# Casting loads behind the selector and masks: a new instruction order at the head of a windowed-attention and MLP kernel

## The chip, the cores and the metric

The kernel runs on one core of one Trainium2 chip. A core has a matrix engine (TensorE, PE in the profile), a vector engine (VectorE, DVE), an activation engine (ScalarE, ACT), GpSimd (POOL) and SyncE (SP), which only starts transfers. ScalarE and GpSimd can start transfers too. The metric is the device time of one execution in microseconds; lower is better.

## The reference

Four batches, 8 heads, 768 positions, head size 64. Attention with a window of 128 and 4 sink positions comes first, then a residual MLP over the rows of 512 values:

```python
scores = scale * np.matmul(q, k.transpose(0, 1, 3, 2))
keep = is_sink | in_window            # in_window: 0 <= row - column < 128
a = softmax(np.where(keep, scores, -1e9)); x = np.matmul(a, v)   # heads side by side: 768 x 512

tok = np.einsum('ts,bsd->btd', w_tok, alpha1 * x + beta1)
u = x + lam * tok
ch = np.maximum((alpha2 * u + beta2) @ w_ch1, 0.0) @ w_ch2       # 512 -> 2048 -> 512
return u + lam * ch
```

Inputs and output are float32; the kernel multiplies in float16.

## The kernel before

The work is cut into some 1,140 tasks, numbered in the order in which the function's body adds them. Three written tables say how they are emitted. `ORDER` lists the task numbers; each engine runs its own share of the list strictly in that order. `ENGINES` has one digit per task for the engine that runs it (0 ACT, 1 DVE, 2 PE, 3 POOL, 4 SP). `HOMES` has one digit per buffer and says in which of the fixed places of its kind it lies: two buffers with one home wait for each other. `IDLES` puts multiplications of a zero tile (`warm`, L148) ahead of some tasks, so that TensorE does not stand idle. Nothing is decided at run time: an instruction waits for its data or its buffer, and all that is queued behind it on its engine waits too.

In batch 0 the order around the change is this, with the names that the profile shows:

- **Loads of q and k.** `load_qk` loads a block of one of q (t = 0) and k (t = 1) for a pair of heads hp (393 KB in float32). Blocks of pair 0 are float32 loads of SyncE (L402, tile `nat`) and are cast by VectorE (`n`, L157). The six blocks of pairs 1 to 3 are in the set `CASTING`: GpSimd starts loads that turn them into float16 on the way (L395). Below, k11 is the k block of pair 1, q10 the q block of pair 1, and so on.
- **Transposes.** `trans` turns a block with TensorE (tile `tp`; L512 for pair 0, L509 for the others; both need the identity `iden`, which GpSimd makes at L330 and L331), and VectorE or ScalarE copies the result into `qkT`.
- **Small constants of GpSimd.** The block masks `mask0` and `maskn` (five selects, L338 to L346), the selector `sel` with the small identity `iden8` (L370, L374), the sink mask `bm` (L359, L363) and `iden`.
- **Scores, sinks and values.** S (L617, L622, L683, L686), the exponential E on ScalarE (L644, L691), sinks `sk` (L554), the products `pv` with v (L716, L723), their division `x` on VectorE (L748, L749), then `xh`, x times `la_b`, on GpSimd (L758).
- **w_tok.** Six loads of SyncE (L440, `wtn`), cast to `wt` on ScalarE or VectorE (L819, L821), transposed (L814, `wT`), used by the token product `tok` (L854). wt_0 is the first of them.
- **w_ch1.** GpSimd loads it in four casting quarters (L453, `w1f`). The hidden layer `h` (L934) multiplies with it: tiles 4 to 7 need the second quarter, 8 to 11 the third, 12 to 15 the fourth. A tiny load, `gates` (L460), makes SyncE wait for a quarter, so that w_ch2 (L449) and the q, k and v of batch 1 come after it.

Later batches repeat attention and MLP, the attention of one batch between the multiplications of the MLP before it.

The functions that start the moved loads are these; the tables themselves are shown with the change.

Of the kernel before, what the change touches and what calls it, by code (L numbers as in the profile page):

```python
# [77 lines left out]
def kernel(  # L78
# [119 lines left out]
    for r in range(NR):  # L198
# [18 lines left out]
        26, 6, 9, 7, 10, 5, 11, 8, 18, 15, 72, 19, 1, 12, 3, 0, 4, 2, 22, 14, 73, 74, 45,  # L217
        48, 46, 17, 39, 49, 47, 53, 13, 40, 50, 41, 90, 95, 43, 91, 51, 54, 103, 52, 16, 44,
        61, 104, 42, 96, 109, 100, 62, 107, 110, 63, 55, 28, 108, 92, 56, 101, 21, 68, 65,
        59, 93, 20, 69, 97, 102, 111, 94, 24, 98, 57, 60, 30, 112, 105, 23, 58, 99, 113,  # L220
        128, 106, 114, 116, 25, 131, 135, 78, 115, 64, 27, 138, 31, 32, 117, 132, 29, 129,
        136, 33, 122, 66, 125, 34, 123, 137, 119, 139, 126, 35, 79, 70, 120, 140, 124, 84,
        71, 80, 133, 130, 141, 67, 146, 85, 134, 121, 147, 144, 75, 118, 158, 86, 154, 148,
        159, 145, 142, 87, 149, 150, 155, 160, 143, 76, 88, 151, 156, 81, 77, 166, 152, 162,
        167, 89, 127, 82, 163, 213, 83, 168, 209, 164, 165, 214, 210, 153, 217, 179, 211,
        178, 157, 197, 229, 36, 212, 215, 218, 185, 216, 226, 230, 219, 176, 161, 177, 220,
        169, 223, 222, 232, 225, 224, 221, 227, 237, 233, 279, 238, 234, 228, 273, 280, 182,
        171, 204, 257, 274, 175, 277, 258, 200, 231, 259, 278, 246, 260, 295, 199, 384, 241,
        248, 188, 186, 291, 296, 247, 172, 243, 289, 174, 181, 242, 293, 292, 187, 170, 290,
        267, 37, 294, 271, 358, 268, 198, 285, 349, 272, 381, 301, 286, 366, 351, 303, 302,  # L230
        189, 297, 378, 173, 304, 281, 180, 352, 203, 249, 190, 282, 298, 379, 250, 287, 380,
        192, 353, 385, 288, 206, 283, 386, 369, 375, 367, 265, 284, 368, 202, 370, 266, 363,
        376, 371, 253, 377, 201, 299, 254, 372, 364, 183, 382, 191, 300, 373, 615, 365, 275,
        374, 383, 357, 261, 276, 408, 262, 387, 263, 184, 409, 205, 195, 239, 411, 264, 410,
        395, 269, 396, 240, 397, 270, 196, 388, 614, 621, 235, 412, 400, 194, 244, 398, 236,
        401, 255, 617, 251, 245, 256, 389, 390, 399, 252, 311, 359, 207, 193, 391, 424, 616,
        335, 425, 393, 341, 426, 392, 336, 648, 427, 634, 413, 394, 312, 636, 414, 428, 419,
        404, 420, 415, 360, 405, 313, 429, 208, 422, 337, 416, 361, 441, 421, 622, 402, 314,
        423, 442, 626, 403, 305, 638, 315, 406, 430, 640, 316, 435, 431, 306, 641, 355, 436,
        443, 619, 437, 338, 649, 618, 438, 362, 317, 432, 637, 407, 307, 433, 345, 444, 339,  # L240
        439, 635, 318, 445, 450, 434, 639, 644, 319, 451, 628, 452, 620, 440, 308, 645, 340,
        453, 417, 446, 323, 447, 418, 320, 309, 448, 324, 321, 658, 322, 329, 449, 642, 659,
        454, 325, 625, 643, 330, 646, 347, 455, 326, 623, 343, 647, 464, 344, 456, 465, 348,
        466, 460, 457, 467, 650, 327, 458, 331, 461, 629, 459, 472, 462, 632, 463, 653, 356,
        651, 656, 627, 332, 38, 654, 480, 333, 342, 624, 652, 473, 310, 476, 468, 471, 470,
        469, 481, 474, 488, 885, 477, 475, 482, 492, 655, 490, 493, 350, 483, 478, 514, 491,
        516, 489, 657, 479, 515, 660, 517, 630, 882, 665, 518, 663, 354, 328, 666, 502, 880,
        661, 664, 498, 879, 519, 508, 499, 346, 503, 678, 662, 512, 509, 679, 504, 513, 487,
        484, 671, 485, 676, 486, 506, 677, 877, 548, 505, 672, 680, 507, 526, 549, 546, 527,
        631, 334, 522, 674, 681, 528, 547, 907, 523, 534, 903, 529, 633, 682, 675, 878, 542,  # L250
        683, 535, 890, 689, 543, 550, 685, 684, 690, 510, 551, 494, 511, 673, 667, 544, 495,
        668, 891, 496, 686, 545, 901, 687, 669, 497, 693, 888, 688, 883, 530, 694, 670, 700,
        531, 524, 897, 701, 698, 500, 691, 525, 696, 699, 552, 501, 697, 704, 553, 558, 695,
        705, 904, 692, 562, 559, 706, 909, 887, 707, 563, 564, 898, 708, 702, 566, 565, 910,
        715, 703, 567, 532, 716, 889, 713, 533, 709, 714, 896, 520, 710, 556, 717, 521, 538,
        557, 537, 540, 539, 536, 560, 541, 899, 718, 921, 572, 922, 881, 711, 574, 884, 573,
        576, 712, 561, 719, 902, 577, 575, 555, 727, 720, 569, 908, 721, 580, 728, 578, 722,
        581, 729, 554, 723, 905, 730, 568, 739, 724, 579, 725, 592, 570, 911, 726, 582, 740,
        593, 588, 912, 583, 595, 584, 571, 906, 743, 589, 731, 585, 900, 590, 732, 605, 744,
        587, 733, 596, 606, 734, 607, 611, 594, 597, 602, 745, 612, 586, 613, 599, 895, 603,  # L260
        591, 757, 765, 600, 758, 601, 759, 766, 741, 771, 760, 742, 916, 772, 751, 917, 746,
        773, 752, 913, 761, 919, 774, 886, 767, 918, 604, 762, 763, 598, 768, 777, 764, 779,
        920, 923, 780, 914, 755, 915, 778, 608, 756, 926, 930, 735, 609, 931, 924, 927, 781,
        736, 925, 775, 782, 737, 928, 753, 929, 893, 738, 934, 754, 892, 769, 935, 932, 610,
        941, 770, 819, 776, 942, 894, 939, 820, 821, 940, 937, 936, 823, 749, 822, 945, 748,
        824, 938, 747, 827, 933, 948, 950, 750, 952, 943, 951, 825, 953, 787, 828, 944, 807,
        788, 797, 826, 808, 949, 946, 829, 798, 801, 954, 830, 791, 802, 956, 947, 792, 783,
        955, 957, 963, 961, 784, 789, 958, 962, 811, 790, 964, 959, 785, 812, 965, 805, 786,
        795, 806, 960, 967, 796, 799, 793, 968, 966, 970, 972, 794, 813, 971, 969, 815, 973,
        814, 809, 800, 816, 803, 810, 974, 978, 804, 976, 979, 837, 975, 977, 835, 838, 980,  # L270
        841, 836, 839, 842, 818, 843, 840, 845, 981, 832, 982, 846, 817, 986, 844, 831, 990,
        987, 983, 988, 847, 991, 984, 851, 833, 992, 1002, 993, 834, 848, 855, 852, 985,
        849, 1003, 859, 856, 1004, 989, 1006, 850, 860, 1005, 853, 998, 1007, 1008, 868,
        999, 857, 1009, 997, 865, 995, 858, 862, 996, 869, 866, 1000, 874, 994, 854, 1001,
        1016, 863, 875, 1040, 1017, 1038, 1041, 1032, 1039, 871, 1020, 872, 1028, 1021,
        1011, 1024, 1029, 1013, 1018, 1033, 1012, 1025, 1034, 1019, 1036, 1010, 1035, 1042,
        1037, 1076, 1043, 1070, 1077, 870, 1074, 1071, 1054, 1075, 1022, 1055, 1060, 1023,
        1048, 1061, 1058, 1049, 1066, 1059, 1014, 1044, 1015, 1067, 1072, 1045, 1056, 1073,
        1026, 1057, 1078, 1068, 1079, 1064, 1069, 1046, 1027, 1050, 1063, 1047, 1052, 1082,
        1053, 1051, 1084, 1083, 1062, 1065, 1030, 1085, 1080, 1101, 1031, 1081, 1091, 1102,  # L280
        1107, 1092, 1097, 1093, 1103, 864, 1108, 1105, 867, 1098, 1111, 1106, 1104, 1113,
        1112, 1089, 1114, 1115, 1086, 1116, 1090, 861, 1094, 1087, 1117, 1099, 1109, 1100,
        1121, 1095, 1110, 1125, 1118, 1122, 1124, 1134, 1126, 1123, 1128, 1135, 1127, 1119,
        1136, 1088, 1140, 1120, 873, 876, 1131, 1129, 1141, 1096, 1137, 1142, 1132, 1130,
        1133, 1138, 1139,
    )
    ENGINES = (
        "3313134433443333444444444444444433334441111201201202120212021213030121211201211210200200"
        "2020201202011202020202020213213213213213213202002020202020213121312131213121312131404444"
        "4044413314433334411114413334444042213221321021020121021021321202020020211212021212020212"  # L290
        "1212020202120212120212020202120202020212122221022221422221022221422221022221013111111131"
        "1311333333302002002102132002132002102020101212010321213120301212131201012121312010121213"
# [17 lines left out]
        "1202002102135312330203"  # L310
    )
    IDLES = (
        (73, 0, 65), (46, 0, 12), (49, 1, 1), (90, 3, 10), (61, 3, 2), (109, 3, 3), (92, 3,
        1), (166, 1, 4), (162, 0, 1),
    )
    W1_SINCE = 20000.0
# [1011 lines left out]
```

## Time and profile before

| what | value |
|---|---|
| time, median of 3 runs | 255.22 us (254.76 to 255.94) |
| the profiled execution's own time | 255.43 us |
| its span, first to last instruction | 253.2 us |
| TensorE busy | 245.4 us, 97% of the span |
| VectorE, ScalarE, GpSimd busy | 190.7, 133.3 and 102.2 us |
| granted TensorE clock | full (1.000) |
| read from memory, written to it | 29.91 MB, 6.29 MB |

The page gives busy time for each engine over the whole span; one line cuts the span in 40 slices and gives each engine's busy share in tenths. The chain of work that ended last follows, from the last instruction back, what released each step. The timeline lists an engine's instructions in order of time: start, length, engine, line, operation, and in brackets how long the engine had been idle and what ended that. "Landing" of a transfer is when its semaphore says that all of it is there.

### The profile page before, as it was taken

The page shows a single profiled execution, that of the slowest core. Times are in us where ns is not written, and L with a number is a line of the kernel's source. Part 1 is how long each engine was busy: PE and PEld are TensorE (multiplying, and loading weights), DVE is VectorE, ACT ScalarE, POOL GpSimd, SP SyncE. Part 2 cuts the span into 40 slices and gives each one's busy share as a digit, 9 for nine tenths or more (in the row PEclk, how much of TensorE's full clock was granted, in tenths as well). Part 3 has the DMA queues.
Part 4 walks back from the last instruction along what each step waited for, and adds up shares of the span by engine and source line. Part 5 has one row for each costly group of instructions (what it writes and reads, how often), then busy time and mean ns, then how long its engine had stood idle before and what let it go on. Part 6 is the DMA issues. An engine that isn't in the chain of part 4 may idle for free.

```text
span 253.2 us, 5499 instructions
## 1 busy us (share of the span) xinstructions
PE 245.4 (97%) x2167; PEld 159.8 (63%) x2167; DVE 190.7 (75%) x402; ACT 133.3 (53%) x219; POOL 102.2 (40%) x124
## 2 busy tenths in 40 slices
PE   8699999999999999999999999999999999999993
PEld 7555646676545544566687686567677676667882
DVE  5588987877788874978879986577778983228892
ACT  2499925879976034787932535566660235543000
POOL 8317854895247417525682040065562220000010
PEclk9999999999999999999999999999999999999999
DMA  6999999999979998997485674420000140100317
GB/s 170 207 240 292 229 276 311 330 362 285 221 130 250 247 194 158 192 244 168 107 176 117 114 151 124 132 66 0 3 0 3 38 83 7 41 0 3 122 70 268
DMA packets 86129, 38.79 MB, mean 153 GB/s; under 512 B 73540, under 2 KB 80460, under 8 KB 86104
## 3 DMA queue, kind: packets, MB, share of 16 engines
q1 hardware_dynamic: 66576, 28.06, 46.9%
q10 hardware_dynamic: 15784, 7.11, 11.9%
q0 software_dynamic: 3744, 3.28, 8.3%
q8 instruction: 17, 0.28, 0.5%
q14 instruction: 8, 0.07, 0.1%
HBM read 29.91 MB, written 6.29 MB: 143 GB/s over the span
## 4 chain that ended last, share of the span: by engine, by line
PE 94%; DMA 3%; DVE 0%; SPq 0%; issue 0%
PE h L934 33%; PE P L1051 22%; PE tok L854 12%; PE ch L1119 8%; PE pv L723 5%; PE S L622 4%; DMA nat<-in_k_dram 3%; PE S L617 2%; PE tp L512 1%; PE pv L716 1%; PE tp L509 1%; PE wT L814 1%; PE sk L554 1%; PE idle L148 1%; PE uTp L895 1%; PE pv L609 1%
## 5 line engine op out<-in xcount | busy, mean ns | idle before, releaser
L934 PE MATMUL h<-uT,w1f 128*128 128x384 f16 x512 | 89.6, 327 | 0.0
L934 PEld LDWEIGHTS <-w1f 128*128 128x128 f16 x512 | 48.2, 98 | 31.0 <-issue 1.7
L940 ACT ACTIVATE hT<-h 128x384 f16<-128x384 f32 x77 | 37.0, 491 | 38.0 <-PE h L934 37.9
L1051 PEld LDWEIGHTS <-hT 128*128 128x128 f16 x408 | 39.4, 98 | 6.8 <-issue 0.2
L942 DVE TENSOR_SCALAR hT<-h 128x384 f16<-128x384 f32 x51 | 27.8, 555 | 20.3 <-PE h L934 19.6
L644 ACT ACTIVATE E<-S 128x1024 f16<-128x1024 f32 (+1 forms) x39 | 38.1, 1002 | 8.1 <-PE S L622 6.6
L767 POOL TENSOR_TENSOR tm<-x,la_b 128x512 f32<-128x512 f32 x18 | 24.3, 1350 | 25.2 <-DVE x L749 13.4
L854 PE MATMUL tok<-xh,wtokT 128*128 128x512 f16 x144 | 33.0, 379 | 0.0
L1064 DVE TENSOR_TENSOR x<-x,P 128x256 f32<-128x256 f32 x45 | 18.3, 419 | 11.3 <-PE P L1051 10.2
L1051 PE MATMUL P<-w2f,hT 128*128 128x256 f16 x216 | 26.5, 273 | 0.0
L854 PEld LDWEIGHTS <-wtokT 128*128 128x128 f16 x144 | 13.9, 98 | 15.0
L1119 PE MATMUL ch<-w2f,hT 128*128 128x512 f16 x96 | 23.2, 380 | 0.0
L1051 PE MATMUL P<-w2s,hT 128*128 128x256 f16 x192 | 23.1, 273 | 0.0
L1087 POOL TENSOR_TENSOR x<-x,pt 128x256 f32<-128x256 f32 x4 | 3.4, 855 | 47.5 <-DVE pt L1082 47.5
L155 ACT CAST u<-x 128x512 f16<-128x512 f32 x15 | 9.2, 615 | 24.9 <-DVE x L861 24.3
L749 DVE TENSOR_TENSOR x<-pv,rec 128x256 f32<-128x256 f32 x48 | 20.4, 425 | 1.7
L155 ACT CAST n<-nat 128x768 f16<-128x768 f32 x21 | 16.9, 828 | 7.4 <-DVE x L1130 6.3
L723 PEld LDWEIGHTS <-E 128*128 128x128 f16 x328 | 14.8, 97 | 5.0 <-issue 1.3
L861 DVE TENSOR_TENSOR x<-x,tok 128x512 f32<-128x512 f32 x24 | 16.0, 683 | 2.4 <-PE tok L854 2.3
L723 PE MATMUL pv<-vfs,E 128*128 128x65 f16 x328 | 17.6, 194 | 0.0
L584 POOL TENSOR_SCALAR_AFFINE_SELECT E<-E 128x512 f16<-128x512 f16 x12 | 7.5, 646 | 21.1 <-ACT E L644 21.1
L748 DVE RECIPROCAL rec<-pv 128x4 f32<-128x4 f32 x48 | 8.6, 179 | 7.7 <-PE pv L723 7.1
(134 smaller groups left out, 339.9 us busy)
## 6 DMA issues: line engine op xcount, KB each, us to landing
wst_w<-in_moe_w_ch_dram SPq DMA_DIRECT2D x8, 512.0 KB, 8.3
nat<-in_q_dram SPq DMA_DIRECT2D x10, 384.0 KB, 4.1
vnat<-in_v_dram SPq DMA_DIRECT2D x14, 256.0 KB, 5.4
nat<-in_k_dram SPq DMA_DIRECT2D x8, 384.0 KB, 6.6
out_dram<-x SPq DMA_DIRECT2D x11, 256.0 KB, 3.1
out_dram<-x ACTq DMA_DIRECT2D x10, 256.0 KB, 3.8
wtn<-in_moe_w_tok_dram SPq DMA_DIRECT2D x6, 384.0 KB, 4.5
w1f<-in_moe_w_ch_dram POOLq DMA_DIRECT2D x4, 512.0 KB, 14.0
```

What stands on the lines that cost most here:

```text
L155: nc.scalar.copy(o, i)
L644: nc.scalar.activation(eT.t, pS.t[:, :, 0 : n * w].rearrange("p e (i w) -> p e i w", i=n), AF.Exp, scale=scale)
L723: nc.tensor.matmul(po.t[:, hl, :], eT.t[:, e_, off + i, c : c + P], vf[j][:, h, :], start=(r < 2 and n == 0), stop=(n == len(parts) - 1 an ...
L749: nc.vector.tensor_mul(bx.t[:, 4 * G : 4 * G + 4, :], po.t[:, :, 0:D], rec.t.to_broadcast([P, 4, D]))
L767: engine[e].tensor_mul(bt.t, bx.t.rearrange("p h d -> p (h d)"), la1_b)
L854: nc.tensor.matmul(pt.t, wtokT[:, si, ti * P : (ti + 1) * P], hs[si].t, start=(si == 0), stop=(si == NR - 1))
L934: nc.tensor.matmul(ph.t, w1f[:, c, fi * P : (fi + 1) * P], bu.t[:, c, chk * NTOK : (chk + 1) * NTOK], start=(c == 0), stop=(c == NC - 1))
L940: nc.scalar.activation(bh.t[:, fi, :], ph.t, AF.Relu)
L942: nc.vector.tensor_scalar_max(bh.t[:, fi, :], ph.t, 0.0)
L1051: nc.tensor.matmul(pc.t, hh[:, nt * P : (nt + 1) * P], w(fi), start=(first and n_ == 0), stop=(n_ == HF - 1), skip_group_check=True)
L1064: nc.vector.tensor_add(row(bx)[:, cols], row(bx)[:, cols], pc.t)
L1119: nc.tensor.matmul(pc.t, bh.t[:, fi, nt * P : (nt + 1) * P], w2f[:, fi, :], start=(fi == 0), stop=(fi == NF - 1))
```

## The change

Only the four tables are changed; `ORDER` is one line shorter, so that lines after it have numbers lower by one. The same tasks are done with the same instructions (4,335 rows in TensorE's list before and after, 99 idle multiplications in both). `IDLES`, (task, home, count), is short enough to show whole, and the head of `ORDER` shows how the first tasks moved:

```diff
-        26, 6, 9, 7, 10, 5, 11, 8, 18, 15, 72, 19, 1, 12, 3, 0, 4, 2, 22, 14, 73, 74, 45,
+        6, 7, 1, 26, 10, 11, 5, 18, 9, 19, 8, 22, 17, 3, 15, 2, 4, 16, 12, 0, 45, 48, 46,
...
     IDLES = (
-        (73, 0, 65), (46, 0, 12), (49, 1, 1), (90, 3, 10), (61, 3, 2), (109, 3, 3), (92, 3,
-        1), (166, 1, 4), (162, 0, 1),
+        (46, 0, 67), (90, 1, 25), (109, 3, 2), (166, 1, 4), (162, 0, 1),
     )
```

(6 and 7 are q and k of pair 0, 26 the first w_tok load, 9, 8, 15, 12, 14 and 13 the casting loads, 1 the masks, 5 the selector, 3 the sink mask, 0 the identity.) What follows from the four tables for each engine:

| queue | before | after |
|---|---|---|
| SP | w_tok 0, q00, k01, v ... | q00, k01, w_tok 0, v ... |
| POOL | k11, sel, q10, k31, masks, q20, bm, iden, q30, k21 | masks, sel, k11, q10, bm, k31, q20, iden, q30, k21 |
| POOL, later | two v casts, xh, w1f x4, xh x11 | la_b product, v cast, xh, v cast, xh x2, v cast, xh, w1f x3, xh, w1f, xh x7 |
| PE | 65 idle, wT0, 12 idle, tp00, 1 idle, tp01, tp11, 10 idle, S, S, tp10, S, 2 idle, tp31, 3 idle, S ... | 67 idle, tp00, tp01, 25 idle, S, tp11, S, tp10, S, wT0, 2 idle, S, S, tp20, ... tp31 ... |
| DVE | cast of wt_0 ahead of the casts of q00 and k01 | casts of q00 and k01 first; wt_0 is cast by ACT |
| SP, batch 1 | k of pairs 3 and 0 started by ACT at 37.44 and 41.80 us | both started by SP, among its other loads after the first gate |

In the float16 buffer of q00 the home is changed too: before it lies where wt_0 was, after it has a place of its own. w_ch2's first block has another home as well and no longer waits for a v cast. The rest, from some 45 us to the end, is many swaps of neighbours: casts and masks that go to another engine (of GpSimd's share there: one w_ch2 product, one bias sum and one q or k cast more, one cast of u fewer), and products that change places.

## The prediction

> **What bounds the kernel now.** I read the page's busy times first, then its chain of waits, then the table of windows, and last the timelines of the first 16 us.
>
> ```profile
> PE 245.4 (97%) x2167; PEld 159.8 (63%) x2167; DVE 190.7 (75%) x402; ACT 133.3 (53%) x219; POOL 102.2 (40%) x124
> ...
> PE 94%; DMA 3%; DVE 0%; SPq 0%; issue 0%
> ```
>
> ```profile
> 0.00:6.30 6.30, 5.15 (x65) 5.03 (x66) 3.46 (x18) 1.28 (x1) 5.09 (x15) 1.00 0.65 170
> 6.30:12.00 5.70, 3.38 (x55) 2.81 (x56) 3.37 (x9) 2.39 (x3) 2.44 (x7) 1.00 1.19 207
> ...
> 45.00:60.00 15.00, 15.00 (x129) 10.15 (x127) 11.25 (x18) 12.83 (x23) 13.42 (x12) 1.00 1.08 341
> 60.00:100.00 40.00, 40.00 (x315) 20.17 (x314) 31.01 (x65) 22.23 (x33) 19.07 (x22) 1.00 1.13 204
> ```
>
> In the second fence the first number after the stretch is its length and the second is TensorE's busy time. From 12 us to the last multiplication at 248.9 us TensorE is busy without a break worth naming; 4.2 us of last sums and stores follow. So nothing after 12 us can be gained on any other engine, only lost. What can be gained lies ahead of the point where TensorE runs without a break:
>
> ```profile
> 7.57 0.50 PE L814 MATMUL wT<-iden,wt 128*128 128x128 f16 x6 [1.37 <-POOL iden L331]
> 7.91 0.83 PE L148 MATMUL idle<-warm 128*128 128x128 f16 x12
> 8.79 0.50 PE L512 MATMUL tp<-iden,n 128*128 128x128 f16 x6
> 9.13 0.22 PE L148 MATMUL idle<-warm 128*128 128x128 f16 x1
> 10.33 0.51 PE L512 MATMUL tp<-iden,n 128*128 128x128 f16 x6 [0.99 <-DVE n L157]
> 10.77 0.53 PE L509 MATMUL tp<-iden,n 128*64 128x128 f16 x12
> 11.23 0.73 PE L148 MATMUL idle<-warm 128*128 128x128 f16 x10
> 11.89 0.39 PE L686 MATMUL S<-qkT 64*128 64x256 f16 x4
> ```
>
> ```profile
> 0.81 0.40 SPq L440
> 1.27 0.41 SPq L402
> 1.72 7.97 DMA nat<-in_k_dram
> 9.71 0.57 DVE n L157
> ```
>
> The second of these is the start of the chain: k01 is asked for at 1.72 us, third behind w_tok and q00, and needs 7.97 us. Its cast ends at 10.27 us, its transpose starts at 10.33 us. Until 14.24 us TensorE's starts hold 3.13 us that aren't work: 0.88 (12 idle ones, 7.91 to 8.79), 1.20 (9.13 to 10.33), 0.66, 0.22 and 0.17 (10, 2 and 3 idle ones).
>
> **What the Trainium skill says.** "DMA: Bandwidth & Descriptors", section "Queues, rings and completion order": each transfer engine goes round between the queues that have work, a packet at a time. The trace agrees: from 30 to 37 us w1f and w_ch2 move 45 to 48 packets each in every 0.5 us. So k01 lost its share when GpSimd's queue began at some 4.2 us: k's packets fell from 115 in a half microsecond (3.5 us) to 28 (4.5 us). Section "Anatomy of one DMA — SWDGE (gpsimd) path" prices a GpSimd load at 2.0 us and its bytes by 436 per ns: 2.9 us for 393 KB. The trace shows 6.6 to 8.9 us for the six of the head, so the price is only the lower end. "TensorE: Matmul & The Clock Gate", section "Back-to-back issue gap", gives N/2.4 GHz and some 2.5 ns from start to start, 56 ns for 128 columns; that fits the idle ones here: 56 ns each, 107 ns for the first 28. Of the change itself no page decides anything.
>
> **The change part by part.**
>
> *Start.* q00 goes out at 0.81 us and k01 at 1.27 us. Before, the second in line (issued at 1.27 us) landed at 5.34 us; I take that for k01. With no GpSimd load moving before some 6.3 us it could be 5.0; at the worst 1.27 + 7.97 = 9.2 us. VectorE's casts follow its copy of bm, due at 5.5 us: 5.5 + 2 x 0.56 = 6.6 us. Both wait for less than `iden` does. On GpSimd the masks take 1.36 us (4.41 to 5.77), sel and iden8 0.63, a load's issue 0.73 (the first 0.90), bm 0.45, the identity 0.57. From 1.40: 1.36 + 0.63 + 0.90 + 0.73 + 0.45 + 2 x 0.73 + 0.57 gives 7.5 us, before 7.52. The same four loads stand ahead of it, so the identity does not move, and tp00 starts at 7.5 us, tp01 at 7.8.
>
> *Up to the first full score tile.* Work between 7.57 and 14.24 us is 6.67 - 3.13 = 3.54 us; tp31 (0.46) now comes later, so 3.08. Idle ones: 25 x 0.056 = 1.40, and 2 for 0.22. So that tile starts at 7.5 + 3.08 + 1.62 = 12.2 us; before it would have without tp31 at 14.24 - 0.46 = 13.78. **Gain 1.6 us.** The 25 idle ones end at 9.55 us; the copy of tp01 (0.54 from start to VectorE, 0.96, 0.2 to TensorE) allows 9.5, so they hide it.
>
> *The casting loads.* k11, q10, k31 and q20 are issued at 3.4, 4.3, 5.5 and 6.2 us, before at 1.31, 2.94, 3.69 and 5.77; each now stands behind five mask selects and sel. TensorE wants k11 at 9.7 us (after S, 0.17) and q10 at 10.85. Ends: price 2.9 us gives 6.3, the longest seen but one (8.3) 11.7. I take 6.0 us, 9.4 and 10.9 to 11.2, since packets came 2.9 us after the issue before and, once k01 was through, at 180 a microsecond; k11 then ended with some 490 packets moved (490/180 = 2.7). q00 and k01, which slowed them before, are gone by then. Cost 0 to 0.4; I take 0.3. k31 has time until 15 us, q20 until 13.8.
>
> *Attention of batch 0.* wt_0's cast moves to ScalarE (0.83), where it lies between two copies; the la_b product (1.22 planned; some 1.3 like the L767 row) to GpSimd, idle from 11.3 to 13.5 us before. v loads are issued no later and meet a quiet queue for 2 us more. S buffers are the next risk: two of them, freed by ScalarE's exponentials of 0.91 us for a PE time of 0.75, but casts of VectorE and ScalarE in between are fewer than before (ScalarE gives up two v casts, 1.45 us, and the copy of wt_0). I cost them at 0 to 0.4, taken 0. tok would start at 31.96 - 1.3 = 30.7 us; the last `xh` that its first part needs (xh3) is due at 29.9 by GpSimd's sum.
>
> *w_ch1.* The quarters go out behind four xh and a third v cast, at some 22.7, 23.5, 24.3 and 25.7 us instead of 21.32 to 23.59. Before they landed at 29.88, 34.28, 38.77 and 44.50. The fourth is used by h tile 15, now after both transposes of u: at 45.62 before, so at 44.3. Transfer engines are full from 25 to 45 us (share 1.09 to 1.15), and bytes that w_ch2's first block moves early, from 25 us on, don't stand in w1f's way later. Before, the gate's answer let SyncE's and ScalarE's loads both in while the fourth quarter still moved; with k31 and k01 on SyncE's queue w1f shares with one queue, not two. I take 42 to 44.4 us: cost 0, up to 0.3. If this cover is gone the price is the fourth issue's full delay, below.
>
> *The rest.* SyncE gets two more issues of 0.4 us, behind the gate, ahead of k21 and w_ch2; all are wanted after 50 us. ScalarE loses them (0.8 us of a queue 53% busy). The swaps of neighbours stay under a TensorE that is never short of work: zero; a gain there is excluded, a loss up to 0.4. The tail is the same 4.2 us.
>
> Sum: -1.6 + 0.3 = -1.3 us on a profiled time of 255.43, 254.1. The median shown is 0.21 below that execution: **253.9 us**.
>
> **The rivals.** (1) *The casting loads are late and eat the gain.* If k11 needs its 8.06 us again it lands at 11.5 us, and TensorE waits 1.7 us behind the first S; the sequence gives back all of it: 255.2, some 254.6 if half. For it: the six landed 1.4 to 1.9 us apart whatever their issue. Against: what slowed the first is gone. (2) *Slower, by w_ch1.* The fourth quarter is issued 2.1 us later (25.7 for 23.59). If it lands that much later and waits also for half of what k31 and k01 add to SyncE's queue (786 KB at the 325 GB/s of 39 to 45 us is 2.4 us, half 1.2), it lands at 47.8 and h tile 15 stops TensorE at 44.3 for 3.5 us: net +2.2, 257.6. It decides from a landing of 45.6 us on, where the gain is gone, and counts as slower by over 0.5% from 46.9. For it: before, the margin was 0.13 us (44.50, first use at 44.63). Against: the transfer engines are full either way, so an issue that is late only changes who goes first. (3) *Nothing to see*, a gain under 0.5 us since S buffers or the last w_tok casts of ScalarE (three before tok) hold PE: 254.9.
>
> **How the numbers follow.** My forecast 0.55 (its own range 253.5 to 254.5), rival 1 0.22, rival 2 0.15, rival 3 0.08. A difference of over 0.5%, 1.28 us, is about what a measurement of this kernel can tell from none, so faster means below 253.94. My forecast lies on that line: I count 0.7 of it as faster, 0.3 as same; rival 1 gives 0.03 faster, the rest same; rival 2 gives 0.12 slower, the rest same; 0.02 slower for what swaps could do. So 0.42 faster, 0.44 same, 0.14 slower. The range runs from 253.2, all of the 1.6 and the noise of the runs shown, to 256.0, which leaves out most of rival 2.
>
> **What would show it.** In the changed kernel's timeline: q00 cast by 6.1 us and k01 by 6.7; tp00 at 7.5 and tp01 directly behind it; first S at 9.5 to 9.7, not 11.89; no idle time named `n<-in_k_dram` or `n<-in_q_dram` above 0.4 us on TensorE; tok at 30.6 to 31; fourth w1f quarter landed before 44.3; TensorE's busy time still 245 us. It is wrong if TensorE has more than 0.5 us idle after 12 us, or if tp00 starts past 8 us.

## The result, and the profile after

| | before | changed |
|---|---|---|
| median (lowest to highest, 4 runs each) | 254.99 us (254.65 to 255.94) | 258.62 us (257.96 to 259.38) |
| profiled execution, its span | 255.43 us, 253.2 us | 259.38 us, 257.7 us |
| TensorE idle ahead of multiplications, 1.06 us before the first among it | 3.5 us | 6.4 us |

The changed kernel is slower: ratio 1.0137, 95% interval 1.009 to 1.0184. The forecast was 253.9 us. The ratio has its interval from the runs; it is not the quotient of the two medians. The first two lines of the page that were shown of before now read:

```profile
PE 247.0 (96%) x2167; PEld 161.1 (63%) x2167; DVE 199.1 (77%) x399; ACT 132.6 (51%) x218; POOL 111.0 (43%) x128
...
PE 73%; POOL 8%; DVE 5%; DMA 4%; ACT 3%; issue 3%; SPq 2%; POOLq 0%; DVEq 0%; ACTq 0%
```

GpSimd is busy 8.8 us longer and VectorE 8.4 us, though VectorE has three instructions fewer, so part of it is that its instructions take longer. The chain that ended last leaves TensorE for 27% of the span, before for 6%. The table of windows of the changed kernel says where (first number: length; second: TensorE's busy time):

```profile
0.00:6.30 6.30, 5.24 (x52) 5.25 (x53) 3.40 (x20) 1.28 (x1) 5.03 (x17) 1.00 0.70 205
6.30:12.00 5.70, 5.20 (x89) 4.23 (x86) 4.23 (x7) 2.90 (x6) 4.12 (x6) 1.00 1.20 201
45.00:60.00 15.00, 15.00 (x130) 9.90 (x129) 11.63 (x19) 12.64 (x24) 11.01 (x12) 1.00 1.08 349
60.00:100.00 40.00, 37.82 (x295) 19.05 (x294) 32.44 (x61) 21.87 (x30) 25.92 (x26) 1.00 1.09 201
100.00:150.00 50.00, 47.96 (x411) 31.17 (x411) 42.92 (x82) 29.08 (x47) 23.01 (x21) 1.00 0.73 150
```

The head did what was forecast, in kind: 5.20 of 5.70 us busy from 6.3 to 12 us, before 3.38. But from 60 to 100 us, where TensorE was busy all 40 us, 2.2 us are missing, and from 100 to 150 us 2.0. Its timeline names the places where TensorE stalls, that is, stands idle, first in the head, then later:

```profile
7.84 0.83 PE L511 MATMUL tp<-iden,n 128*128 128x128 f16 x12 [0.50 <-POOL iden L330]
8.51 1.56 PE L148 MATMUL idle<-warm 128*128 128x128 f16 x25
10.00 0.28 PE L685 MATMUL S<-qkT 64*128 64x256 f16 x2
...
12.93 0.27 PE L148 MATMUL idle<-warm 128*128 128x128 f16 x2 [0.38 <-DVE qkT L157]
...
65.18 0.81 PE L933 MATMUL h<-uT,w1f 128*128 128x384 f16 x4 [0.25 <-DVE hT L941]
...
68.35 0.20 PE L722 MATMUL pv<-vfs,E 128*128 128x65 f16 x1 [0.73 <-POOL E L583]
69.36 0.37 PE L722 MATMUL pv<-vfs,E 128*128 128x65 f16 x7 [0.81 <-POOL vfs L157]
...
100.34 0.61 PE L621 MATMUL S<-qkT 64*128 64x256 f16 x8 [0.73 <-ACT E L643]
...
130.84 1.03 PE L1050 MATMUL P<-w2f,hT 128*128 128x256 f16 x8 [1.17 <-DVE pt L157]
...
138.79 1.38 PE L1050 MATMUL P<-w2f,hS 128*128 128x256 f16 x11 [0.53 <-DVE hS L991]
```

Since the orders differ, I compare the traces at equal work: each multiplication counts its columns, idle ones nothing, the total is the same in all kernels, and the table gives how much later (+) or earlier (-) than before TensorE has done the same sum. The rows are named by the time at which before gets there.

| at (before's time) | changed | gp12_right | tail_back | prod_back |
|---|---|---|---|---|
| 11.9 us | -1.11 | -1.10 | -1.11 | -1.10 |
| 31.4 us | -1.57 | -1.55 | -1.56 | -1.56 |
| 43.7 us | -1.04 | -1.00 | -1.03 | -1.04 |
| 61.9 us | -0.99 | -0.94 | -0.97 | -0.99 |
| 73.0 us | +1.22 | -1.02 | -0.24 | -0.98 |
| 97.2 us | +1.02 | -1.22 | -0.22 | -0.95 |
| 108.4 us | +2.05 | -0.20 | -0.21 | -0.95 |
| 125.9 us | +2.04 | -0.20 | -0.21 | -0.95 |
| 138.3 us | +4.19 | -0.20 | -0.22 | -0.95 |
| 246.5 us | +4.47 | +0.08 | -0.21 | -0.95 |

So the changed kernel gains 1.57 us, gives back 0.53 at 30 to 39 us, and then loses 5.5: 2.2 at 62 to 73 us, 0.8 net at 85 to 108, 2.15 at 126 to 138, 0.28 at 186. The other three columns are experiments.

Each column is one execution, and so is before. Where TensorE takes its products in another order, a row can be off by 0.2 us, and the execution of before was not one of its shortest (255.43 us, median 254.99). Two more traces have before's head, gp12_only and prod_in_before below. In them VectorE casts k01 at 9.08 and 9.19 us, not at 9.71, and the first S starts at 11.26 and 11.37 us, not at 11.89: half of the first row is how late k01 happened to land in the one execution from which the forecast was worked out. By 31.4 us these two (both long executions) are 0.4 and 0.9 us behind before's trace. So the head's gain, read against a single trace of before, can be out by more than half a microsecond.

### The profile page after: what moved, and what is told of

It is laid out like the page before. It is cut to its first block, busy times and chain, and to the rows that moved or that the text cites. A ratio compares the mean times of both kernels' runs of the same rounds, so it can differ in the third digit from the quotient of the medians.

```text
span 257.7 us, 5516 instructions
## 1 busy us (share of the span) xinstructions
PE 247.0 (96%) x2167; PEld 161.1 (63%) x2167; DVE 199.1 (77%) x399; ACT 132.6 (51%) x218; POOL 111.0 (43%) x128
## 3 DMA queue, kind: packets, MB, share of 16 engines
q1 hardware_dynamic: 67120, 28.85, 46.7%
## 4 chain that ended last, share of the span: by engine, by line
PE 73%; POOL 8%; DVE 5%; DMA 4%; ACT 3%; issue 3%; SPq 2%; POOLq 0%; DVEq 0%; ACTq 0%
PE h L933 22%; PE P L1050 20%; PE tok L853 12%; PE ch L1118 7%; PE pv L722 4%; DMA wst_w<-in_moe_w_ch_dram 3%; PE S L621 3%; POOL w2f L835 2%; POOL E L583 2%; SPq L401 1%; ACT E L643 1%; PE S L616 1%; POOL n L394 1%; DMA vnat<-in_v_dram 1%; ACT wt L818 1%
## 5 line engine op out<-in xcount | busy, mean ns | idle before, releaser
L939 ACT ACTIVATE hT<-h 128x384 f16<-128x384 f32 x78 | 37.3, 491 | 40.2 <-PE h L933 39.8
L941 DVE TENSOR_SCALAR hT<-h 128x384 f16<-128x384 f32 x50 | 27.0, 553 | 19.5 <-PE h L933 17.4
L766 POOL TENSOR_TENSOR tm<-x,la_b 128x512 f32<-128x512 f32 x18 | 25.2, 1400 | 22.8 <-DVE x L748 12.3
L155 ACT CAST n<-nat 128x768 f16<-128x768 f32 x20 | 16.3, 829 | 7.8 <-DVE xh L769 5.9
L658 DVE TENSOR_TENSOR E<-E,maskn 128x1024 f16<-128x1024 f16 x18 | 15.7, 874 | 0.2 <-ACT E L643 0.2
L583 POOL TENSOR_SCALAR_AFFINE_SELECT E<-E 128x512 f16<-128x512 f16 x12 | 9.2, 789 | 15.1 <-ACT E L643 15.1
```

Of the source, the lines that this page charges most:

```text
L155: nc.scalar.copy(o, i)
L766: engine[e].tensor_mul(bt.t, bx.t.rearrange("p h d -> p (h d)"), la1_b)
L939: nc.scalar.activation(bh.t[:, fi, :], ph.t, AF.Relu)
L941: nc.vector.tensor_scalar_max(bh.t[:, fi, :], ph.t, 0.0)
```

## The experiments

All were timed against before on the same chip in the same session; its median there was 255.7, 254.75, 254.92, 254.96 and 255.08 us in the five sessions, so ratios are to be compared, not times. A second measure is a kernel's lowest time less before's lowest in its session, since that hardly moves: 254.09, 254.10, 254.14, 254.17 and 254.07 us. In the first four kernels the written tables take more lines, so their line numbers are up to eight higher. Tasks are named by number: 372 is the cast of batch 1's k block of pair 1, 194 a product of w_ch2 with `lam_b` (w2f), 353 a difference of two w2f blocks (w2s), 377 ScalarE's copy of a transposed block, 684 a mask of batch 2, 718 a bias sum of batch 2 (`xh`), 660 an S product of batch 2.

### GpSimd's later edits, undone and done alone

gp12_back, the changed kernel with

```diff
-  372: POOL, 194: POOL, 718: POOL; POOL: ... 202, 353 ...; ... 669, 684 ...
+  372: ACT,  194: DVE,  718: DVE;  POOL: ... 190, 353 ...; ... 633, 684 ...
```

> The changed kernel with GpSimd's five late edits undone: the q or k cast of batch 1 back on ScalarE, the w_ch2 product back on VectorE, the bias sum of batch 2 back on VectorE, the w_ch2 difference (w2s) and one mask of batch 2 back in their places in GpSimd's queue. Theory (GpSimd's load after 50 us is the loss): the stalls at 65 to 69 us (2.2 us) and at 129 to 139 us (2.1 us) go, those at 99.6 and 105 us (1.0) stay: 258.6 - 4.3 = 254.3, ratio 0.997. Rival (the stalls come from TensorE's own new order or from the head): both stalls stay within 0.5 us, about 258, ratio 1.012.

Measured 255.69 us, ratio 0.9996 (0.997 to 1.0022). The stalls at 65 to 69 and at 129 to 139 us are gone, the one before S stays (0.73 us): the five edits make these stalls. But a ratio of 0.997 was expected, 0.7 us less. A stall of 0.37 us stands at 57 us that the changed kernel doesn't have, and costs 0.53 at equal work.

gp12_only, the kernel before with the same five edits:

> The kernel before with those five edits alone. Theory: +2.2 and +2.1 us less what TensorE's later arrival hides (it comes 1.04 us later than in the changed kernel, so up to 1.0 of the first stall can be hidden if GpSimd's queue doesn't move with it): 257 to 259.3 us, ratio 1.008 to 1.017. Rival: within 0.5 us of before, ratio 1.000 to 1.002.

Measured 259.82 us, ratio 1.015 (1.0089 to 1.021): without any change in the head, the five edits cost about what the changed kernel lost. Its profiled execution was 2.9 us above its median, so I read only names from it: 2.5 us behind GpSimd's cast of n, 1.27 before P behind `pt`, 0.75 before hS. In before's order the cast stands behind a product and a difference that it precedes in the changed kernel, so the run shows that such a load on GpSimd costs, not how much of it was the change's.

gp1_back, the changed kernel with 372, 194 and 353 alone as before:

> The changed kernel with only the three edits of 50 to 70 us undone (cast and product of GpSimd back on ScalarE and VectorE, w2s in its old place). Theory: the stall at 65 to 69 us goes and the one at 129 to 139 us stays: 258.6 - 2.2 = 256.4, ratio 1.006. Rival (the later stall is only a consequence of the first, or grows by what the first gives back): 254.3 or 258.6.

Measured 258.15 us, ratio 1.0102 (1.0066 to 1.0137), not 1.006. The later stalls are there in full (1.17 and 0.54 us), so they don't hang on the first. The first is gone, but stalls of 0.19 and 0.82 us at 55 to 58 us have taken its place: again that new stall.

### The head alone

head_only takes the changed kernel's first 246 tasks, then before's rest:

> The changed kernel's order up to some 45 us (its first 246 tasks, with their engines and buffers), then the order, engines and buffers of the kernel before. Theory (the head gives its gain, what was lost comes from the edits after 50 us): TensorE is 1.04 us ahead of the kernel before at 45 us and stays so: about 254.0 us, ratio 0.996. Rival (the head's gain itself brings TensorE early to data that is not earlier, so the stall at 67 to 69 us comes with the head): a stall of 1 us or more at 60 to 70 us, 255.0 or more.

Measured 260.24 us, ratio 1.0177 (1.0137 to 1.0217), worse than either kernel, and for a reason of its own: the two assignments of buffers don't fit. In the mix, two w_ch2 blocks that SyncE loads one behind the other share a place, and its queue issues nothing from 46.7 to 57.0 us. Up to 61 us TensorE is 1.02 us ahead, as in the changed kernel, and has no stall at 57 us; on what follows this run says nothing. late_back joins the two at a point where both kernels have emitted the same tasks:

```diff
-  ORDER, ENGINES, HOMES: the changed kernel's, to the end
+  gp1_back's for the first 396 tasks (to some 83 us), then before's
```

> The changed kernel up to some 83 us (its first 396 tasks), with GpSimd's three edits of batch 1 undone as in gp1_back, then the kernel before. Theory (the swaps after 85 us cost 0.76 and 0.27 at 98 to 105 us, 2.1 at 129 to 139, 0.28 at 186, each by itself): TensorE's lateness against before stays from 60 us on where gp1_back had it there, between -0.5 and +0.3 us: 255.2 to 256.0 where before is 255.7, ratio 0.998 to 1.001. Rival (the later stalls come from what is upstream): stalls of over 1 us in all after 85 us, 257 or more.

Measured 254.65 us, ratio 0.9994 (0.9973 to 1.0016). Nothing is lost after 58 us: all that the changed kernel loses behind 85 us, 3.2 us at equal work, comes from its late swaps. But the head's 1.0 us is gone at the one place at 57 us (ScalarE's and TensorE's timeline of late_back):

```profile
56.12 0.83 ACT L155 CAST n<-nat 128x768 f16<-128x768 f32 x1 [0.33 <-DMA nat<-in_k_dram]
56.86 0.79 ACT L155 COPY qkT<-tp 128x768 f16<-128x768 f16 x1
...
57.70 1.00 PE L511 MATMUL tp<-iden,n 128*128 128x128 f16 x15 [0.79 <-ACT qkT L155]
```

ScalarE waits for the last k block of batch 1, which landed at 56.0 us, casts it, and only then copies the transposed block for which TensorE waits. I first read this as a limit: that block landed at 55.86 us in before too, so a head that is 1 us ahead would gain nothing. That reading was wrong. In the kernel before, the copy (377) stands ahead of the cast (372) on ScalarE. In the changed kernel the cast comes earlier in the list, which does no harm while GpSimd does it; back on ScalarE, in gp12_back, gp1_back and late_back, it stood in front of the copy. The correction:

```diff
 ACT (undo_right, from late_back; gp12_right, from gp12_back)
-  363, 372, 377
+  363, 377, 372
```

> late_back once more, with one thing put right in how the edits were undone: the cast of the last k block of batch 1 stands on ScalarE behind the copy of a transposed block, as in the kernel before; in late_back, gp1_back and gp12_back it stood ahead of that copy. Theory A (the stall at 57 us in those three came from that place alone): no stall of over 0.2 us at 55 to 58 us, the head's 1.0 us is kept, ratio 0.996. Theory B (batch 1's data, which land no earlier, meet a head that is 1 us ahead, whatever the order): a stall of 0.5 us or more at 55 to 62 us, ratio 0.998 to 1.001.

Measured 254.3 us, ratio 0.9977 (0.9961 to 0.9994). There is no stall at 57 us. The gain is less than the 0.996 expected. The profiled execution was 1.1 us above the median; it had 0.38 us at 40 us for a w1f quarter and 0.47 at 66 us, and TensorE reached 57 us only 0.4 us ahead, which makes this the weaker of the two tests.

> gp12_back with the same correction: the changed kernel with GpSimd's five late edits undone and the cast behind the copy. Theory A: 0.6 us under gp12_back, only the S product's 0.8 and the 0.28 us at 186 us are lost of the head's 1.0: ratio 0.997 to 1.000. Theory B: as gp12_back, 0.9996 or above.

Measured 255.36 us, ratio 1.0015 (0.9997 to 1.0033). The ratio misses theory A's 0.997 to 1.000 and lies where theory B had it; the trace decides for A. TensorE has only two stalls after 40 us, 0.73 us before S at 98 us and 0.11 at 182, stays 1.0 us ahead to 85 us, and ends 0.08 behind before. The lowest times agree: against before's lowest, the correction takes late_back from +0.41 to -0.07 us and gp12_back from +1.46 to +0.97. So the place of one cast ahead of one copy cost 0.5 to 1.0 us at equal work in the traces (gp12_back, late_back) and 0.5 in the lowest times, and the data of batch 1 do not take the head's gain away.

tail_back leaves GpSimd's three edits of batch 1 in, and takes before's rest:

> The changed kernel up to some 83 us (its first 396 tasks as they are, GpSimd's cast and product of batch 1 included), then the kernel before. Theory: TensorE is 1.0 us ahead at 55 us, has no stall at 57 us (the last k block of batch 1 is cast by GpSimd as it lands), but 1.5 to 2.2 us of stall at 65 to 69 us behind GpSimd's masks, and nothing after: +0.5 to +1.2 us against before, 255.3 to 256.0, ratio 1.002 to 1.005. Rival (the tail is not a cause by itself): stalls after 85 us, 258.

Measured 255.59 us, ratio 1.0009 (0.9987 to 1.0032). As expected there is no stall at 57 us and none after 70. But the one at 67 us is 0.65 us in this execution, where 1.5 to 2.2 were expected, and the ratio lies under the expected 1.002 to 1.005.

### Which of GpSimd's edits

prod_back is tail_back with one engine and one place changed:

```diff
-  194: POOL; POOL: ... 202, 353 ...
+  194: DVE;  POOL: ... 190, 353 ...
```

> tail_back with only the w_ch2 product back on VectorE and the w2s difference back in its old place; the cast of the last k block of batch 1 stays on GpSimd. Theory (the cast on GpSimd frees ScalarE's queue at 56 us, and without the product of 1.6 us GpSimd's masks come in time): no stall of over 0.3 us at 55 to 70 us, TensorE stays 1.0 ahead: ratio 0.996. Rival (the cast alone, which holds GpSimd until the block lands at 56 us, is enough to delay the masks): a stall of 0.5 us or more at 65 to 69 us, ratio 0.999 to 1.003.

Measured 254.41 us, ratio 0.9963 (0.9943 to 0.9983): faster than both kernels, and in the trace the head's 0.95 us reach the end. In the times the gain is smaller: 0.5 us in the medians (254.92 for before), and the lowest times, 254.04 and 254.14, hardly differ. So the head shows its gain in the usual execution, not in before's shortest ones; of those there is no trace, and why they are as short stays open. GpSimd's queue in the changed kernel and then in prod_back:

```profile
56.33 0.83 POOL L157 CAST n<-nat 128x768 f16<-128x768 f32 x1 [2.60 <-PE h L933]
57.71 1.27 POOL L835 TENSOR_TENSOR w2f<-wst_w,lam_b 128x512 f16<-128x512 f32 x1 [0.56 <-DMA wst_w<-in_moe_w_ch_dram]
58.93 0.61 POOL L157 CAST vfs<-vnat 128x512 f16<-128x512 f32 x1
59.50 1.27 POOL L835 TENSOR_TENSOR w2f<-wst_w,lam_b 128x512 f16<-128x512 f32 x1
60.72 1.60 POOL L965 TENSOR_TENSOR w2s<-w2f 128x512 f16<-128x512 f16 x1
62.29 1.82 POOL L835 TENSOR_TENSOR w2f<-wst_w,lam_b 128x512 f16<-128x512 f32 x1
64.06 4.24 POOL L583 TENSOR_SCALAR_AFFINE_SELECT E<-E 128x512 f16<-128x512 f16 x4
68.25 1.06 POOL L157 CAST vfs<-vnat 128x512 f16<-128x512 f32 x1
```

```profile
58.61 2.94 POOL L835 TENSOR_TENSOR w2f<-wst_w,lam_b 128x512 f16<-128x512 f32 x2
61.51 1.68 POOL L583 TENSOR_SCALAR_AFFINE_SELECT E<-E 128x512 f16<-128x512 f16 x2
63.68 2.21 POOL L583 TENSOR_SCALAR_AFFINE_SELECT E<-E 128x512 f16<-128x512 f16 x2 [0.49 <-ACT E L643]
65.85 1.06 POOL L157 CAST vfs<-vnat 128x512 f16<-128x512 f32 x1
```

In the changed kernel the difference (1.60 us) and one product stand ahead of the masks (L583), which start without a pause at 64.06 us and run to 68.3; the v cast behind them ends at 69.3, and TensorE's wait of 0.73 us ends with the masks, that of 0.81 us with the cast. In prod_back the four masks are over at 65.9 us, the v cast at 66.9, and TensorE asks at 67.0.

prod_only_back is the changed kernel with the same one edit:

> The changed kernel with only the w_ch2 product back on VectorE and the w2s difference in its old place; everything else as changed. Theory (as prod_back showed, the product is what makes GpSimd's masks late): the stall at 65 to 69 us goes, 0.7 to 2.2 us by the traces of the changed kernel and of tail_back: 256.4 to 257.9, ratio 1.006 to 1.012. Rival (with later w1f landings the masks are late without it): a stall of 0.5 us or more at 65 to 69 us.

Measured 257.79 us, ratio 1.0109 (1.0081 to 1.0138); no stall at 65 to 69 us, all the later ones as in the changed kernel. And the kernel before with that product alone on GpSimd, prod_in_before:

> The kernel before with the one w_ch2 product on GpSimd and the w2s difference at its later place, and nothing else. If the product is too much for GpSimd's 4.1 us of idle time there whatever the head does: a stall of 0.3 us or more at 65 to 70 us, ratio 1.001 to 1.004. If it is too much only with a head that is 1 us ahead, or only together with the cast on GpSimd: within 0.2 us of before, ratio 1.000.

Measured 255.38 us, ratio 1.0003 (0.998 to 1.0026). Without the new head and without the cast the product costs nothing that can be measured, though the interval doesn't exclude a cost of up to 0.7 us. The trace (2.7 us above the median) agrees: GpSimd still idles 1.56 and 1.61 us ahead of the masks. The one stall there, 0.33 us at 70.5 us, ends with a v cast that had waited 1.99 us for its load. Which of the two makes the product too much was not separated.

### Loads, tried while the stall at 57 us was misread

w1_early and w1_k_act, both from late_back:

```diff
 POOL (w1_early)
-  64, 118, 130, 66, 127, 32, 33, 34     (32 to 35: w1f)
+  64, 32, 33, 118, 130, 66, 127, 34
 (w1_k_act, besides)
-  171: SP, 177: SP
+  171: ACT, 177: ACT
```

> late_back with the first two w1f quarters asked for 3.3 us earlier, behind the second v cast of GpSimd, some 20.0 and 20.8 us. Theory A (the first gate, which waits for the second quarter, holds SyncE's loads of batch 1, and these make the stall of 0.6 to 1.3 us at 55 to 58 us): the gate answers at some 34 us, not 36 to 37.3, no stall of over 0.2 us at 50 to 62 us, TensorE ends some 1.0 us ahead of before: ratio 0.996. Rival B (the transfer engines are full either way and batch 1's blocks land at the same time whatever the order): stall and time as in late_back, ratio 0.998 to 1.001.

Measured 256.97 us, ratio 1.0086 (1.0057 to 1.0115). It doesn't decide what it was made for: the first gate answered at 35.3 us, and a new stall of 1.71 us came at 22.3 to 24.0 us, where VectorE's copies into `ks` came late. With the k block landed at 54.8 us there was still 0.37 us of stall, up to 59.1 us.

> w1_early with k of pairs 3 and 0 of batch 1 started by ScalarE again, at its old places between ScalarE's casts of u and h. If those two loads' move to SyncE cost something (eight issues in SyncE's queue behind one gate): 0.3 to 1 us under w1_early. If not: within 0.3 us of w1_early, or above it where ScalarE's issues come late.

Measured 258.9 us, ratio 1.0185 (1.0144 to 1.0226). Against w1_early it is 2.0 us later at equal work; 0.8 of that falls at 38 to 50 us (0.29 us of it a named wait for ScalarE's cast of u), the rest before the moved loads are issued. The gain of 0.3 to 1 us that a price of the two moves would have brought did not come; the 1.2 us ahead of the loads can't be theirs.

k11_early and k11_prod ask for the last k block (173) earlier, in late_back and in prod_back:

```diff
-  SP: 171, 186, 172, 174, 170, gate, 198, 173
+  SP: 171, 173, 186, 172, 174, 170, gate, 198
```

> late_back with the load of batch 1's last k block (pair 1) asked for by SyncE ahead of a w_ch2 block, two q blocks more, the second gate and another w_ch2 block, some 43 us instead of 47.5. Theory (that block lands at 56.0 us whatever the head does, ScalarE's cast of it stands ahead of the copy for which TensorE waits at 56.9 us): it lands before 54 us, that stall of 0.8 to 1.0 us goes, TensorE stays 1.0 ahead: 253.7 where before is 254.75, ratio 0.996. Rival (the transfer engines are full: another block, now later, stops TensorE instead): a stall of 0.5 us or more with another name at 52 to 64 us, ratio 0.998 to 1.001.

Measured 255.14 us, ratio 1.0004 (0.9985 to 1.0023). The block was there at 49.4 us, 6.7 us earlier, and TensorE still waited 0.36 us for ScalarE's copy behind the cast, and 0.19 us for a cast of GpSimd. So the landing was not the main cause.

> prod_back with the earlier load of k11_early. If both theories hold: the same as the better of the two, ratio 0.995 to 0.996, since there is only the 1.0 us of the head to keep. If another transfer is late: as in k11_early's rival.

Measured 254.23 us, ratio 0.9979 (0.9959 to 0.9999); in the profiled execution 0.62 us of stall for ScalarE's cast at 55.2 us. Not better than prod_back.

### The later stalls, one by one

```diff
 mask_back    POOL: -  669, 684       +  633, 684
 bias_back    -  718: POOL            +  718: DVE
 s_back       PE: -  332, 660, 472    +  472, ..., 516, 660
```

> The changed kernel with one thing undone: GpSimd's mask of batch 2 (pair of tile 3) back ahead of the v cast and product in its queue; the bias sum stays on GpSimd. Theory (the mask's move puts GpSimd's products and sum beside VectorE's masks at 126 to 130 us and slows these): the 1.17 us stall before P at 129.7 goes, the 0.53 us one before hS stays: 258.6 - 1.4 = 257.2, ratio 1.006 against 255.7. Rival (the bias sum on GpSimd does it): the stall stays, 258.6, ratio 1.011.

Measured 257.38 us, ratio 1.0116 (1.0082 to 1.015). (The 1.006 expected was taken against another session's median; 257.2 against this one's 254.75 is 1.0096.) The 1.17 us stall is gone (1.43 us at equal work), the 0.54 us before hS stays. VectorE in the changed kernel, then two instructions of GpSimd beside it, then VectorE in mask_back:

```profile
126.66 2.29 DVE L658 TENSOR_TENSOR E<-E,maskn 128x1024 f16<-128x1024 f16 x2
128.88 1.57 DVE L769 TENSOR_TENSOR xh<-tm,lb_b 128x512 f16<-128x512 f32 x1
130.37 0.74 DVE L157 COPY pt<-P 128x256 f32<-128x256 f32 x2
...
126.54 1.26 POOL L766 TENSOR_TENSOR tm<-x,la_b 128x512 f32<-128x512 f32 x1
128.60 1.30 POOL L583 TENSOR_SCALAR_AFFINE_SELECT E_None<-E_None 128x1024 f16<-128x1024 f16 x1 [0.80 <-ACT E_None L643]
```

```profile
125.99 1.28 DVE L658 TENSOR_TENSOR E<-E,maskn 128x1024 f16<-128x1024 f16 x2
127.19 0.69 DVE L769 TENSOR_TENSOR xh<-tm,lb_b 128x512 f16<-128x512 f32 x1
127.81 0.42 DVE L157 COPY pt<-P 128x256 f32<-128x256 f32 x1
```

The same three instructions take 3.86 us in one and 1.97 in the other, and TensorE waits for the copy behind them. In the changed kernel GpSimd's product (126.54 to 127.80 us) and its next mask (128.60 to 129.90) lie beside them; in mask_back the product is over by 126.08 and that mask starts at 127.93. The Trainium skill says why, "SBUF — State Buffer", section "Who interferes with whom": a VectorE instruction with two inputs in that memory and a GpSimd instruction that reads it share a port, and who comes second waits until the first is done. The numbers fit. In mask_back a mask takes 0.68 us and a sum 0.69. A first mask that is held until 127.80 and then takes 0.68 ends at 128.48 (measured 128.36), a sum that is held until 129.90 and then takes 0.69 at 130.59 (130.45): both 0.1 us early.

> The changed kernel with only the bias sum of batch 2 back on VectorE. Theory (it slows the S3 difference of h beside it, and the mask's move does the rest): the 0.53 us stall before hS at 138 us goes, the 1.17 us one at 129.7 stays: 258.6 - 0.7 = 257.9, ratio 1.012. Rival (VectorE's sum of 0.68 us itself delays hS by as much): no change, ratio 1.0145.

Measured 257.61 us, ratio 1.0108 (1.0078 to 1.0139). The stall before hS is gone (0.72 us at equal work), though VectorE now has the sum. Its two differences hS in the changed kernel with GpSimd's sum beside them, and in bias_back:

```profile
134.90 3.83 DVE L991 TENSOR_TENSOR hS<-hT,hT 128x1536 f16<-128x1536 f16 x2 [0.33 <-ACT hT L939]
136.06 1.86 POOL L769 TENSOR_TENSOR xh<-tm,lb_b 128x512 f16<-128x512 f32 x1
...
133.46 2.76 DVE L991 TENSOR_TENSOR hS<-hT,hT 128x1536 f16<-128x1536 f16 x2 [0.33 <-ACT hT L939]
```

The first of the two lies beside a product of GpSimd in both runs and takes 1.89 us in both; the second takes 2.02 us beside the sum and 0.94 without it. The sum itself takes 1.86 us there, where such a sum of GpSimd takes 1.28 in before (122.09 us).

> The changed kernel with one thing undone on TensorE: the second S of batch 2 back behind three token products and five h tiles, where the kernel before has it. Theory (moved ahead of the token products, it waits for an S buffer that ScalarE's exponential still reads): the 0.73 us stall at 99.6 us goes, with it 0.76 us; the stalls at 65 to 69 and 129 to 139 us stay: 258.6 - 0.8 = 257.8, against before 254.9 a ratio of 1.011. Rival (the later masks and products take that time anyway): 258.6, ratio 1.0145.

Measured 258.29 us, ratio 1.0133 (1.0097 to 1.017). The 0.73 us stall is gone, 0.65 us at equal work; against the spread of the runs the time alone doesn't show it.

By the traces, GpSimd's product with the two edits around it (0.78 in tail_back), the S product (0.65), the mask (1.43) and the bias sum (0.72) make 3.6 us of the loss of 5.5. In the changed kernel's own profiled execution the product cost 1.4 more: GpSimd's masks began at 64.06 us, in tail_back at 62.59. Loads were later there. The last k block landed at 56.18 us (54.80 in tail_back), so 372 started 0.61 us later, and GpSimd then waited 0.56 us for a w_ch2 block, in tail_back not at all. mask_back lies between (stalls of 1.25 us): 372 starts there as in tail_back, but the w_ch2 block is late by 0.32 us. s_back and bias_back, which have the same edits up to there, repeat tail_back's 0.65 us. So the product costs 0.8 us at equal work in three traces of five, and up to 2.2 where loads are late. The 0.28 us at 186 us, where VectorE's division was put elsewhere, was not tried by itself.

## Why the prediction was wrong

**Start and head: right in kind, too good in size.** The identity came 0.3 us later than worked out (tp00 at 7.84, not 7.5 us; its memset took 0.53 us, in before 0.20), the 25 idle multiplications covered VectorE's copy, and the first S stood at 10.00 us, not 9.5 to 9.7. The first full score tile came at 13.04 us; forecast 12.2, or 12.5 with the cost of the loads. k11 landed at 9.00 us (forecast 9.4), q10 at 10.94 (10.9 to 11.2), with no wait for either. That the 0.3 us taken for them were lost all the same is luck: they went to VectorE, 0.38 us for the copy of a transpose, behind VectorE's `lb_b` product and shuffle (9.58 to 12.0 us). q00's and k01's casts ended at 7.3 us, not by 6.7, still ahead of the identity. (In the trace of before, w1f and w_ch2 move 44 to 55 packets in half a microsecond from 30.5 to 37 us, not 45 to 48, as the prediction read; that they share evenly stands.)

**To tok: right, in part by luck.** It starts at 30.74 us; forecast 30.7, in the band of 30.6 to 31. From 14 to 22 us TensorE was only 0.4 to 1.0 us ahead at equal work; what brought the rest by 30 us was not looked into. Of the 1.57 us, 0.35 go in the last w_tok transposes, which wait for ScalarE's casts: the mechanism of rival 3, at a third of its size.

**w_ch1: right, but narrow.** The fourth quarter landed at 42.65 us (forecast 42 to 44.4), and rival 2's mechanism did not happen. But the step followed only the fourth. The second, whose landing opens SyncE's first gate, came at 37.27 us instead of 34.28, and SyncE's loads for batch 1 began 3.0 us later. With the same issue time it landed anywhere from 35.3 to 38.1 us in the runs with this head. At the early end it cost nothing: in prod_back and gp12_right (gates at 35.4 and 35.5 us) TensorE has no stall above 0.05 us from 31 to 90 us. At the late end it did: in undo_right's profiled execution (38.1) a late quarter held TensorE for 0.38 us. In the changed kernel's (37.3) the place with the product lost 2.2 us and not 0.8; but in mask_back, with the earliest gate (35.3), it lost 1.6, so the gate alone doesn't decide that.

**The rest: this is the step that failed.** It read: "The swaps of neighbours stay under a TensorE that is never short of work: zero; a gain there is excluded, a loss up to 0.4." In the profiled execution it was 5.5 us, and TensorE stood idle for 4.9 us after 12 us, where the prediction had named over 0.5 as a sign of being wrong. I took 97% busy for slack on the other engines, and counted no instruction of these edits. The trace of before had the numbers: GpSimd's idle times ahead of the batch 1 masks, and the exponential that the moved S product would meet.

```profile
61.80 1.31 POOL L584 TENSOR_SCALAR_AFFINE_SELECT E<-E 128x512 f16<-128x512 f16 x2 [2.48 <-ACT E L644]
64.72 1.29 POOL L584 TENSOR_SCALAR_AFFINE_SELECT E<-E 128x512 f16<-128x512 f16 x2 [1.61 <-ACT E L644]
...
99.32 1.02 ACT L644 ACTIVATE E<-S 128x1024 f16<-128x1024 f32 x1
```

The product (1.27 us), the difference (1.15 in before, where it stands ahead of this stretch) and the cast (0.83) take 3.25 of the 4.09 us, and a TensorE that comes 1.0 us earlier leaves nothing; this is an estimate from these lengths. The product's price depends on what else is moved (prod_in_before), so it was to be taken with the cast and the earlier head, not by itself. The S product that was moved ahead of the token products wanted at 99.6 us a buffer that ScalarE's exponential held until 100.3 us in before too. And the two pairs of instructions, masks beside a product and the second hS beside a sum, stand one behind the other in before and lie side by side after.

**The sum.** Forecast -1.3; measured -1.04 at 45 us against the one trace of before, of which nothing is left at the end. That a gain was to be had, prod_back shows: 0.95 us in its trace, 0.5 in the medians. So the head's term was too large as well, in part because it was worked out from an execution in which k01 landed late; but it is the term of the swaps, 5.5 us for zero, that turned a gain into a loss.

## What to carry to other kernels

A TensorE that never waits says that nothing beside it is worth speeding up; it doesn't say that there is room there. Before a swap is priced at nothing, take the idle time of its queue ahead of the next instruction with a deadline, and subtract all that is moved in together, with a two-input instruction of VectorE and an instruction of GpSimd that come to lie beside each other priced as if they stood in one queue. Before a gain is worked out from one trace of before, ask how much its weakest wait varies from execution to execution. And an edit is undone only when its place in the queue is undone too: a cast that waits for a load, one place ahead of a copy that TensorE needs, cost 0.5 to 1.0 us here, as much as the head gained.

## What the runs showed that I had not expected

TensorE's first idle multiplications take 107 ns and later ones 56 ns, and when that turns differs from execution to execution: after 26 of them in undo_right, 2.75 us from the first one, after 27 in before (2.9 us), after 47 (5.0 us) in the changed kernel, after 57 (6.0 us) in k11_prod. The Trainium skill, "TensorE: Matmul & The Clock Gate", section "Part 1: The HAM clock gate (the "warmup" mystery)", gives some 3.4 us, and says that it varies with the phase of a window that runs by itself; here it is 2.75 to 6.0 us. In the changed kernel it cost nothing, since the identity came later still, but it makes 1.0 of the 1.6 us by which TensorE's busy time grew.
